# v scaled by a maximum and kept as two float16 parts, and x of some chunks handed over through DRAM, in a fused attention and two-MLP kernel

## The chip, the cores and the metric

One core of a Trainium2 chip runs the whole program. The metric is device microseconds (us) from start to end of one execution; lower is better. Of the kernel before there are three runs: a median of 1001.1 us, between 998.04 and 1001.42.

## What is computed

The reference, cut to what matters:

```python
# attention: 4 batches, 8 heads, 576 positions, 64 per head; causal
scores = q @ k.T / 8
bias = -(cum[:, :, :, None] - cum[:, :, None, :])      # cum: running sum of max(s, 0)
scores = where(causal, -1e9, scores + minimum(bias, 0))
attn = softmax(scores)
x = (attn @ v), laid out as [2304 tokens, 512]
# first MLP, 2048 wide
r = maximum(x @ w_in, 0)
x = (s * r * r + b) @ w_out
# second MLP, 1536 wide
out = ((x @ w_a) * (x @ w_b)) @ w_out2
```

All inputs of the products are float32 or float64; the kernel splits them into high and low parts and multiplies the parts, three terms to a float32 product (high x high, high x low, low x high).

## The kernel before

**Stages.** The 2304 tokens are nine chunks of 256. Chunks 0 to 3 are the first 256 positions of the four batches ("first halves"), chunks 4 to 7 the next 256 ("second halves"), chunk 8 the last 64 positions of all four batches, which are worked out with the second halves. Attention makes x of a chunk (`first_half`, `second_half`, each ending in `value_product`). The first MLP takes x: `h_unit` multiplies by w_in, `elementwise` squares, `y_unit` multiplies by w_out, chunk by chunk; chunks 7 and 8 go together with 512 columns (`last_two`). Attention of later chunks is laid between the MLP's matmuls of earlier ones. When the first MLP is done, the second MLP follows (`x_pair`, `group`, `conv`, then `g_pair`, `g_conv`).

**One value product.** A pair of heads is one product: first halves have two key blocks, second halves five. Probabilities are scaled by 32768 (PSC) and kept as two float16 parts; v is kept as three bfloat16 parts, so that their sum has v's digits. `split_v` (L356) makes them: cast, subtract, cast, subtract; the casts run on POOL for first halves and on ACT (ScalarE) for second halves, the subtractions on DVE, in place in the buffer of raw v (`rv`). `value_product` (L562) sums five terms per key block and head: three parts of v with the high part of the probabilities, two with the low part. The result lies in a bank of the tag `t_s`, the pool of four PSUM banks that scores use as well, and ACT and DVE write it out as a high and a low part of x.

**x.** `x_all` has two slots of four pairs; chunk c uses slot c mod 2, so a value product of chunk c can only run when the MLP has read chunk c − 2 (`room=[xt]`). x of chunk 8 is collected in DRAM (`xl_dr`) and read back (L825).

**What sets the order.** All work is declared with `op(engine, cost, position, ...)`. `Plan.order` (L122) replays the declared costs and positions and puts out one fixed order per engine; a buffer is given when its turn in its tag comes. On the chip each engine then works through its list in order. A DMA stands in the list of SP, which issues all of them; a waiting instruction holds up all behind it on its engine. `light_pos` (L410) gives the positions of first halves, the call of `second_half` at 130 + 78b + 19p those of the second halves. The rest of the tables here are the tags, with their number of buffers:

```python
t_h = tag(ps_mm, [P, 512], F32, 2, "h", in_order=False)      # banks of h
t_s = tag(ps_at, [P, 512], F32, 4, "s", in_order=False)      # banks of scores and value products
t_r = tag(moe, [P, 2, N], F32, 2, "r", in_order=False)       # between h and its split
t_rv = tag("att1", [P, 5, 2, D], F32, 1, "rv")               # raw v of a second half
t_vt = tag("att1", [P, 5, 2, 3, D], BF16, 1, "vt")           # its parts
```

Of the kernel before, what the change touches and what calls it, by code (L numbers as in the profile page):

```python
# [22 lines left out]
PSC = 32768.0  # L23
G_ACT = (0, 1)
# [211 lines left out]
def fused_kernel(  # L236
# [66 lines left out]
    xl_dr = dram_buf([NPAIR, P, 2, N], F32R, "xl_dr")  # L303
    y_dr = dram_buf([(NCK + 1) // 2, KC, P, 2 * N], F32, "y_dr")
# [7 lines left out]
    x_slots = iter([x_all[:, ck % 2, c] for ck in range(NCK) for c in range(KC)])  # L312
    t_x = Tag(lambda n: next(x_slots), 2 * KC)
    t_xl = tag(moe, [P, 2, SL], F32R, 2, "xl")
# [4 lines left out]
    def make_const():  # L319
        nc.gpsimd.memset(as32(ident), 0.0)  # L320
# [14 lines left out]
    mask2 = atc.tile([P, SL], F32R, name="mask2")  # L335
    sb_s = const.tile([P, 1], F32, name="sb_s")
# [12 lines left out]
    t_vt0 = tag("att0", [P, 2, 2, 2, 3, D], BF16, 2, "vt")  # L349
# [3 lines left out]
    t_sm0 = {n: tag("att0", [P, 4], F32, 3, n) for n in ("nm", "sm", "rc")}  # L353
    t_raw = tag("att0", [P, 2, DM, 2], U32, 1, "rl")

    def split_v(v3, rv, eng, cost, sub, pr):  # L356

        buf, ap = v3
        rvb, rap = rv
        cast = nc.gpsimd.tensor_copy if eng == POOL else nc.scalar.copy  # L360
        ops = []
        for i in range(2):
            ops.append(op(eng, cost, pr, lambda i=i: cast(ap(i), rap()), r=[rvb], w=[(buf, i)]))
            if i == 0:
                op(DVE, sub, pr, lambda: nc.vector.tensor_tensor(out=rap(), in0=rap(), in1=ap(0), op=ALU.subtract),
                   r=[(buf, 0)], w=[rvb])
        op(DVE, sub, pr, lambda: nc.vector.tensor_tensor(out=ap(2), in0=rap(), in1=ap(1), op=ALU.subtract),
           r=[rvb, (buf, 1)], w=[(buf, 2)])
        return ops

    light = {}
    casts = []
# [4 lines left out]
    def light_load(i, in_w):  # L377
# [6 lines left out]
        light[i] = kq, rv, vt  # L384
# [8 lines left out]
        def ones():  # L393
# [3 lines left out]
        op(POOL, 1.9, pr, ones, w=[(kq, "o0"), (kq, "o1")], behind=casts[2 * i - 3 : 2 * i - 2])  # L397
# [10 lines left out]
        casts.extend(split_v((vt, lambda a: vt.t[..., a, :]), (rv, lambda: rv.t), POOL, 0.63, 0.7, light_pos(i) + (0.5 if i else 2.6)))  # L408
# [116 lines left out]
    x_t = {}  # L525

# [35 lines left out]
    def value_product(b, half, p, vt, vap, tr, pr):  # L562
# [4 lines left out]
        ap = Buf(t_s, f"av{b}{half}{p}")  # L567
        xt = x_t[b + B * half, p]
# [28 lines left out]
    def first_half(i):  # L597

        b, g = divmod(i, 2)
        kq, rv, vt = light[i]  # L600
# [5 lines left out]
        for x in range(2):  # L606
            p = 2 * g + x
            pr = light_pos(i) + 2.5 * x
            x_t[b, p] = Buf(t_x, f"xs{b}{p}")
# [5 lines left out]
            for ti in (1, 0):  # L615
# [15 lines left out]
                op(PE, 2 * (w / 600 + 0.08), pr, go, r=[kq, masks], w=[bank], late=0.15, room=[hl])  # L631
                op(DVE, DVE_PS(2 * w), pr, lambda at=at, nmx=nmx, view=view: nc.vector.tensor_reduce(
                    out=nmx.t[:, at : at + 2], in_=view(), axis=AX.X, op=ALU.max, negate=True
                ), r=[bank], w=[(nmx, ti)])
                tiles[ti] = w, bank, at, view, hl
            op(DVE, 0.17, pr, lambda nmx=nmx: nc.vector.tensor_scalar_mul(nmx.t, nmx.t, SCALE), w=[nmx])
            pts = {}
            for ti in (1, 0):
                w, bank, at, view, hl = tiles[ti]
                for h in range(2):  # L640
# [5 lines left out]
                    ), r=[bank, nmx], w=[pt, (sm, at + h)], late=0.1)  # L646
# [10 lines left out]
            value_product(b, 0, p, vt, lambda j, h, vi, x=x: vt.t[:, x, j, h, vi, :], tr, pr + 1.0)  # L657
# [15 lines left out]
    barrier.tags = {t_kq0, t_rv0, t_vt0, t_p0, t_tr0, t_raw, *t_hl0.values(), *t_sm0.values()}  # L673
# [27 lines left out]
    t_vt = tag("att1", [P, 5, 2, 3, D], BF16, 1, "vt")  # L701
# [6 lines left out]

    def second_half(b, p, pos):
# [27 lines left out]
        split_v((vt, lambda a: vt.t[..., a, :]), (rv, lambda: rv.t), ACT, 0.7, 0.82, pos + 0.9)  # L737
# [17 lines left out]
        for z, ti in enumerate(("L", 1, 0)):  # L755
# [6 lines left out]
            for c in range(2):  # L762
                def go(c=c, ti=ti, w=w, bank=banks[c]):
# [18 lines left out]
                op(PE, 0.56 if ti == "L" else 2 * (w / 2400 + 0.014) + 0.08, pr, go, r=[sets, masks], w=[banks[c]], late=0.15,  # L782
                   room=[hl])
# [750 lines left out]
```

## Time and profile before

| | |
|---|---|
| median of 3 runs | 1001.1 us |
| profiled execution | 998.96 us, its span 997.2 us |
| PE (TensorE) busy | 968.4 us, 97% of the span |
| weight loads (PEld, beside PE) | 871.5 us, 87% |
| DVE (VectorE) | 707.4 us, 71% |
| ACT (ScalarE) | 548.9 us, 55% |
| POOL (GpSimd) | 108.5 us, 11% |
| DMA | 160.12 MB, mean 161 GB/s |

Busy time is a share of the whole span, over stages that differ. Matmuls are pipelined and their ends are modelled, so PE's share is not its distance from its peak. The chain followed back from the last instruction says what set the end; what an engine costs is read from the stage in which the work stands.

### The profile page before, as it was taken

To read this page: it belongs to the slowest core of one execution; us is meant where nothing else is said; L and a number is where in the kernel's file an instruction comes from. 1 tells how busy PE (TensorE), PEld (TensorE's weight loads), DVE (VectorE), ACT (ScalarE), POOL (GpSimd) and SP (SyncE) were. 2 spreads that over 40 slices of the span, in tenths; PEclk is the share of its full clock that TensorE was granted. 3 is DMA by queue.
4 is the path that set the end of the run, shared out by engine and by line. 5 is a ranking of instruction groups with operands and counts; after the bars stand their busy time and mean duration, and the time that the engine had idled before them with its cause. 6 is when DMAs were issued, how large, how long until landed. Compare 5 with 4: busy or idle time off the path is not lost.

```text
span 997.2 us, 17243 instructions
## 1 busy us (share of the span) xinstructions
PE 968.4 (97%) x6664; PEld 871.5 (87%) x6664; DVE 707.4 (71%) x1151; ACT 548.9 (55%) x1025; POOL 108.5 (11%) x135
## 2 busy tenths in 40 slices
PE   5798999999999999999999999999999999999998
PEld 4698999999999999999988887888888888888888
DVE  6887644578888788888576627778688776878852
ACT  4788984568778777777463423344253421334431
POOL 4121000100000000000001004133143311000000
PEclk9999999999999999999999999999999999999999
DMA  9969423457776858777560103446366556977013
GB/s 240 231 164 227 163 82 79 113 128 141 168 148 157 172 128 165 159 153 146 106 226 1 63 24 125 156 147 247 137 240 228 187 185 260 377 307 253 22 65 104
DMA packets 159249, 160.12 MB, mean 161 GB/s; under 512 B 115008, under 2 KB 126016, under 8 KB 153280
## 3 DMA queue, kind: packets, MB, share of 16 engines
q1 hardware_dynamic: 159168, 159.03, 55.9%
q8 instruction: 52, 0.85, 0.4%
q14 instruction: 29, 0.24, 0.1%
HBM read 95.20 MB, written 37.52 MB: 133 GB/s over the span
## 4 chain that ended last, share of the span: by engine, by line
PE 92%; DMA 3%; DVE 2%; ACT 1%; issue 0%; POOL 0%; SPq 0%; DVEq 0%; POOLq 0%; ACTq 0%
PE b L1100 21%; PE y L882 16%; PE h L862 15%; PE pb L1324 11%; PE av L577 6%; PE hh L915 4%; PE yy L927 4%; PE bc L1100 3%; PE s L627 3%; PE s L779 3%; PE pbc L1384 2%; DMA raw<-in_w_dram 2%; DMA tr<-hl 1%; DVE x1d L1035 1%; PE s L628 0%; DMA yr<-y_dr 0%
## 5 line engine op out<-in xcount | busy, mean ns | idle before, releaser
L882 PE MATMUL y<-g,w 128*128 128x256 f32 x1344 | 183.6, 286 | 1.8 <-ACT p L643 1.8
L862 PE MATMUL h<-x_all,w 128*128 128x256 f32 x1344 | 179.0, 285 | 2.7 <-ACT x_all L588 2.1
L862 PEld LDWEIGHTS h<-x_all,w 128*128 128x128 f32 x1344 | 167.8, 192 | 4.4 <-ACT x_all L588 2.3
L882 PEld LDWEIGHTS y<-g,w 128*128 128x128 f32 x1344 | 167.9, 191 | 3.5 <-ACT p L643 2.0
L577 PE MATMUL av<-tr,vt 128*64 128x320 f16 (+4 forms) x1120 | 64.8, 273 | 9.1 <-DMA tr<-hl 9.1
L1100 PE MATMUL b<-x,wa 128*128 128x512 f32 x288 | 72.8, 390 | 0.0
L577 PEld LDWEIGHTS <-vt 128*64 128x64 bf16 x1120 | 54.3, 115 | 20.2 <-issue 6.6
L541 ACT ACTIVATE hl<-p,rc 128x256 f16<-128x256 f32 (+3 forms) x128 | 65.5, 558 | 10.7 <-DVE rc L558 6.9
L543 DVE SCALAR_TENSOR_TENSOR hl<-p,rc,hl 128x256 f16<-128x256 f32 (+3 forms) x128 | 65.5, 549 | 1.6 <-ACT hl L541 1.3
L1100 PEld LDWEIGHTS b<-x,wa 128*128 128x128 f32 x288 | 53.6, 188 | 11.3 <-ACT su L1135 0.5
L842 DVE SCALAR_TENSOR_TENSOR r<-r,sb_s 128x512 f32<-128x512 f32 x40 | 30.0, 750 | 37.8 <-ACT r L831 37.8
L1100 PE MATMUL b<-x1d,ws 128*128 128x512 f32 x216 | 54.1, 390 | 0.6 <-DVE su L1125 0.5
L1100 PE MATMUL b<-x0d,ws 128*128 128x512 f32 x216 | 53.7, 389 | 0.0
L627 PE MATMUL s<-kq 66*128 66x256 f32 (+1 forms) x128 | 42.4, 458 | 10.2 <-DMA kq<-sums 7.8
L1324 PE MATMUL pb<-g,wo 128*128 128x512 f32 x216 | 50.7, 390 | 0.0
L1100 PEld LDWEIGHTS b<-x1d,ws 128*128 128x128 f32 x216 | 40.4, 188 | 9.7 <-DVE su L1125 1.4
L1324 PEld LDWEIGHTS pb<-g,wo 128*128 128x128 f32 x216 | 40.4, 188 | 8.7 <-DVE g L1272 0.4
L1100 PEld LDWEIGHTS b<-x0d,ws 128*128 128x128 f32 x216 | 40.4, 188 | 8.3
L463 DVE SCALAR_TENSOR_TENSOR raw<-raw 128x1024 uint32<-128x1024 uint32 x28 | 34.9, 1245 | 17.1 <-ACT raw L457 14.2
L831 ACT ACTIVATE r<-h 128x512 f32<-128x512 f32 x56 | 33.5, 598 | 24.1 <-PE h L862 22.1
L1125 DVE TENSOR_TENSOR su<-b,su 128x512 f32<-128x512 f32 x48 | 33.0, 688 | 17.9 <-PE b L1100 17.7
L915 PE MATMUL hh<-x_all,w 128*128 128x512 f32 x192 | 45.7, 389 | 0.0
(380 smaller groups left out, 1881.3 us busy)
## 6 DMA issues: line engine op xcount, KB each, us to landing
raw<-in_w_dram SPq DMA_DIRECT2D x16, 1024.0 KB
raw<-in_w2ab_dram SPq DMA_DIRECT2D x12, 1024.0 KB
ab_dr<-at_all SPq DMA_DIRECT2D x24, 512.0 KB
R<-ab_dr SPq DMA_DIRECT2D x24, 512.0 KB
wo<-wo_dr SPq DMA_DIRECT2D x12, 1024.0 KB
rk<-in_k_dram SPq DMA_DIRECT2D x16, 576.0 KB
raw_o<-in_w2o_dram SPq DMA_DIRECT2D x6, 1024.0 KB
wo_dr<-wao SPq DMA_DIRECT2D x24, 256.0 KB
```

Of the source, the lines that this page charges most:

```text
L463: op(DVE, 1.15, pr, lambda: nc.vector.scalar_tensor_tensor(out=hi(), in0=hi(), scalar=3, in1=lo(), op0=ALU.logical_shift_left, op1=ALU.bit ...
L541: nc.scalar.activation(o, i_, AF.Copy, scale=r_)
L543: nc.vector.scalar_tensor_tensor(out=o, in0=i_, scalar=r_, in1=place()[:, k0:k1, 0, :cols], op0=ALU.mult, op1=ALU.subtract)
L577: nc.tensor.matmul(ap.t[64 * h : 64 * h + 64, :w], vap(j, h, vi), t[:, j, a, h, :w], start=j == 0 and m == 0, stop=j == nkt - 1 and m == 4,)
L627: nc.tensor.matmul(o, qt[:66, x, h, ti * P : (ti + 1) * P], kt[:66, x, h, :w], start=True, stop=False)
L831: op(ACT, 0.49, e, lambda: nc.scalar.activation(r.t.rearrange("p a n -> p (a n)"), hp.t, AF.Relu), r=[hp], w=[r], late=0.1)
L862: nc.tensor.matmul(o, w[:, wi, c, :], x_t[ck, c].t[:, xi], start=m == 0, stop=m == 3 * KC - 1)
L882: nc.tensor.matmul(o, w1_t[2 * fp + j].t[:, 1, wi, e * P : (e + 1) * P], g.t[:, gi, j], start=fp == 0 and e % 2 == 0 and j == wi == gi == ...
L915: nc.tensor.matmul(hp.t, w[:, wi, c, :], x_all[:, :, c, xi, :], start=m == 0, stop=m == 3 * KC - 1)
L927: nc.tensor.matmul(y_ps[e].t, w1_t[f].t[:, 1, wi, e * P : (e + 1) * P], g.t[:, gi].rearrange("p a n -> p (a n)"), start=f == m == 0, stop= ...
L1100: nc.tensor.matmul(o, wt.t[:, q, wi, kt * P : (kt + 1) * P], hl_of(kt, xi), start=first and n == 0, stop=last and n == 5, skip_group_check ...
L1324: nc.tensor.matmul(banks[bi][dp].t, wv(i2, wi, dp), hl.t[:, i2, xi, :], start=n_ in fresh and ip == i2 == m == 0, stop=ip == NIP - 1 and i ...
```

## The change

**Scale and parts of v.** For each block of v, DVE takes the largest absolute value in each partition; one float32 matmul with a matrix of 1/32768 (`ones`) adds these over the partitions and puts the sum into every partition, in column 511 of a score bank; three small DVE operations make of it the factor for v, and the factor that goes back on when x is written out. v times the factor is kept as two float16 parts (one cast, one subtraction), and a value product sums three terms: high x high, low x high, high x low.

**Where value products of second halves go.** Into a bank of `t_h` and no longer of `t_s`.

**x.** Pairs outside the set `DIRECT` (all of chunks 2, 3 and 7, pairs 1 to 3 of chunk 4, pair 3 of chunk 6: 16 pairs) are written into an `r` buffer, from there to DRAM (`xs_dr`), and read into their slot when it is free. x of chunks 7 and 8 has a tile of its own (`x_end`), in space that attention leaves at its end, and is read back from DRAM by eight loads. The raw weights of the second MLP take the space of `x_all` instead.

**Positions.** First halves 4 to 7 stand at 44 + 12(i − 4) (50 + 14(i − 4) before), second halves at 110 + 80b + 19p (130 + 78b + 19p before). The work of chunks 7 and 8 is declared matmul group by matmul group, in the same count and shape.

The diff, cut to its core:

```diff
+VSC = 32768.0
-    x_slots = iter([x_all[:, ck % 2, c] for ck in range(NCK) for c in range(KC)])
+    x_slots = iter([x_all[:, ck % 2, c] for ck in range(NCK - 2) for c in range(KC)])
...
+    t_xe = Tag(end_slot, 2 * KC)
...
+        nc.gpsimd.memset(ones, 1.0 / VSC)
...
-    t_vt0 = tag("att0", [P, 2, 2, 2, 3, D], BF16, 2, "vt")
+    t_vt0 = tag("att0", [P, 2, 2, 2, 2, D], F16, 2, "vt")
...
+    def scale_v(vs, mx, rv, bank, n, pr):
+
+        op(DVE, DVE_1(n) + 0.25, pr, lambda: nc.vector.tensor_reduce(
+            out=mx.t, in_=rv[1](), axis=AX.X, op=ALU.max, apply_absolute_value=True
+        ), r=[rv[0]], w=[mx])
+        col = slice(511, 512)
+        op(PE, 0.1, pr, lambda: nc.tensor.matmul(bank.t[:, col], ones, mx.t, start=True, stop=True, skip_group_check=True),
+           r=[mx, masks], w=[(bank, "v")], late=0.1)
+
+        def go():
+            nc.vector.tensor_scalar_max(vs.t[:, 0:1], bank.t[:, col], 1e-30)
+            nc.vector.reciprocal(vs.t[:, 1:2], vs.t[:, 0:1])
+            nc.vector.tensor_scalar_mul(vs.t[:, 2:3], vs.t[:, 0:1], 1.0 / PSC)
+
+        op(DVE, 0.5, pr, go, r=[(bank, "v")], w=[vs])
+
-    def split_v(v3, rv, eng, cost, sub, pr):
+    def split_v(v2, rv, vs, eng, cost, sub, pr):
...
+            if eng == POOL:
+                nc.gpsimd.tensor_scalar(ap(0), rap(), vs.t[:, 1:2], None, op0=ALU.mult)
+            else:
+                nc.scalar.activation(ap(0), rap(), AF.Copy, scale=vs.t[:, 1:2])
+
+        op(DVE, sub, pr, lambda: nc.vector.scalar_tensor_tensor(
+            out=ap(1), in0=rap(), scalar=vs.t[:, 1:2], in1=ap(0), op0=ALU.mult, op1=ALU.subtract
+        ), r=[rvb, vs, (buf, 0)], w=[(buf, 1)], after=[c := op(eng, cost, pr, cast, r=[rvb, vs], w=[(buf, 0)])])
...
-        return 0.0 + 5.0 * i if i < 2 else 14.0 + 9.0 * (i - 2) if i < 4 else 50.0 + 14.0 * (i - 4)
+        return 0.0 + 5.0 * i if i < 2 else 14.0 + 9.0 * (i - 2) if i < 4 else 44 + 12 * (i - 4)
...
+    DIRECT = {(ck, p) for ck in range(NCK - 2) for p in range(NPAIR)} - {(2, 0), (2, 1), (2, 2), (2, 3), (3, 0), (3, 1), (3, 2), (3, 3), (4, 1), (4, 2), (4, 3), (6, 3)}
...
-        ap = Buf(t_s, f"av{b}{half}{p}")
-        xt = x_t[b + B * half, p]
+        ck = b + B * half
+        away = (ck, p) not in DIRECT
+        ap = Buf(t_h if half else t_s, f"av{b}{half}{p}")
+        xt = Buf(t_r, f"xw{ck}{p}") if away else x_t[ck, p]
...
-                for m, (vi, a) in enumerate(((0, 0), (1, 0), (2, 0), (0, 1), (1, 1))):
+                for m, (vi, a) in enumerate(((0, 0), (1, 0), (0, 1))):
...
+        if away:
+            op(SP, 0.4, pr, lambda: nc.sync.dma_start(as32(xs_dr.t[ck - 2, p]), xt.t), r=[xt], w=[(xs_dr, (ck, p))], dma=262144)
...
+                scale_v(vs, mx, (rv, lambda: rv.t.rearrange("p c h d -> p (c h d)")), banks[0], 640, pos + 0.15)
+                split_v((vt, lambda a: vt.t[..., a, :]), (rv, lambda: rv.t), vs, ACT, 0.7, 0.82, pos + 0.9)
...
-            second_half(b, p, 130.0 + 78.0 * b + 19.0 * p)
+            second_half(b, p, 110 + 80 * b + 19 * p)
...
+        op(SP, 0.4, pr, lambda: nc.sync.dma_start(as32(x_t[ck, p].t), as32(xl_dr.t[p] if last else xs_dr.t[ck - 2, p])),
+           r=[xl_dr if last else (xs_dr, (ck, p))], w=[x_t[ck, p]], dma=262144)
```

Names in the rows below: `hC_F`, `yC_E` are the MLP's products of chunk C; `av` with batch, half and pair is a value product; `s` with half, batch, pair and tile a score bank (`L` is the block of the last 64 positions); `mx` the new maximum; `rv`, `tr`, `raw` are raw v, transposed probabilities and raw w1.

PE's order around the first scores of second half (batch 1, pair 0), before:

```order
L862 MATMUL h3_5_3538<-x_all_82,w1_10_1310 128x256 x12
L769 MATMUL s110L0_3556<-K0_2414,Q0_2413 128x288 x2
L769 MATMUL s110L0_3556<-K1_2416,Q1_2415 128x288 x2
L769 MATMUL s110L1_3564<-K0_2414,Q0_2413 128x288 x2
L769 MATMUL s110L1_3564<-K1_2416,Q1_2415 128x288 x2
L775 MATMUL s110L1_3564<-mask2_85,ident_83 128x64
L882 MATMUL y3_1_3229<-g3_2_3227,w1_4_601 128x256 x3
L882 MATMUL y3_1_3229<-g3_2_3227,w1_5_896 128x256 x3
L862 MATMUL h3_5_3538<-x_all_82,w1_11_1458 128x256 x12
```

and in the change:

```order
L934 MATMUL h3_4_3376<-x_all_83,w1_8_1164 128x256 x12
L827 MATMUL s110L0_3401<-K0_2223,Q0_2222 128x288 x2
L827 MATMUL s110L0_3401<-K1_2225,Q1_2224 128x288 x2
L827 MATMUL s110L1_3402<-K0_2223,Q0_2222 128x288 x2
L827 MATMUL s110L1_3402<-K1_2225,Q1_2224 128x288 x2
L833 MATMUL s110L1_3402<-mask2_86,ident_84 128x64
L934 MATMUL h3_4_3376<-x_all_83,w1_9_1317 128x256 x12
L954 MATMUL y3_0_3177<-g3_2_3236,w1_4_775 128x256 x3
L954 MATMUL y3_0_3177<-g3_2_3236,w1_5_942 128x256 x3
L376 MATMUL s110L0_3401<-mx110_3434,ones_87 128x1
L954 MATMUL y3_1_3187<-g3_2_3236,w1_4_775 128x256 x3
L954 MATMUL y3_1_3187<-g3_2_3236,w1_5_942 128x256 x3
```

The value product `av012` stands four `y3` products (2.88 us) ahead of the first row; the new matmul on `mx110` stands behind the scores, an h product and six `y3` matmuls, and the rest of PE's list behind it.

SP's order around the load of v for batch 0, pair 3 (`rv103`), before:

```order
L594 DMA xl_dr_80<-xl01_3244 256x1x64
L718 DMA rq110_3296<-in_q1_dram 128x704
L749 DMA_TRANSPOSE tr102_3224<-hl1020_2949 128x12x128
L719 DMA rv103_3339<-in_v_dram 128x640
L720 DMA Q1_2415<-aug_q_78 2x2x320
L723 DMA K1_2416<-aug_k_79 2x2x576
```

and in the change:

```order
L640 DMA xs_dr_81<-xw41_2961 128x512
L642 DMA xl_dr_80<-xl01_3014 256x1x64
L801 DMA_TRANSPOSE tr102_3066<-hl102L_2900 128x10x64 x2
L888 DMA x_all_83<-xs_dr_81 128x512
L778 DMA rv103_3102<-in_v_dram 128x640
L777 DMA rq110_3104<-in_q1_dram 128x704
L776 DMA rk110_3113<-in_k_dram 128x1152
```

The load of v now stands behind the write of a pair of x to DRAM and directly behind a reload of x.

SP's order at the fourth and fifth loads of w1, before:

```order
L653 DMA_TRANSPOSE tr002_352<-hl0021_193 128x8x128
L653 DMA_TRANSPOSE tr002_352<-hl0020_206 128x4x128
L448 DMA raw4_375<-in_w1_dram 128x2048
L520 DMA aug_q_78<-sums_hl_275 16x2x64
L520 DMA aug_q_78<-sums_hl_275 16x2x256
L400 DMA kq4_394<-in_kl_dram 64x1024
L400 DMA kq4_394<-in_ql_dram 64x1024
L448 DMA raw3_432<-in_w1_dram 128x2048
```

and in the change:

```order
L433 DMA rv04_453<-in_v_dram 128x2x256
L437 DMA kq4_328<-sums_107 1x4x256 x2
L432 DMA kq5_477<-in_kl_dram 64x1024
L709 DMA_TRANSPOSE tr010_488<-hl0101_355 128x8x128
L709 DMA_TRANSPOSE tr010_488<-hl0100_372 128x4x128
L432 DMA kq5_477<-in_ql_dram 64x1024
L433 DMA rv05_536<-in_v_dram 128x2x256
L437 DMA kq5_477<-sums_107 1x4x256 x2
L709 DMA_TRANSPOSE tr011_575<-hl0111_383 128x8x128
L709 DMA_TRANSPOSE tr011_575<-hl0110_431 128x4x128
L479 DMA raw3_608<-in_w1_dram 128x2048
L479 DMA raw4_610<-in_w1_dram 128x2048
```

These two loads of w1 now stand behind the transposes of three more pairs (`tr003`, which is just ahead of the rows, `tr010` and `tr011`) and behind the loads for `kq5`.

## Rows read from the trace of the kernel before

**Rows 1.** The page: its part 1, and the chain of part 4 by line.

```profile
PE 968.4 (97%) x6664; PEld 871.5 (87%) x6664; DVE 707.4 (71%) x1151; ACT 548.9 (55%) x1025; POOL 108.5 (11%) x135
...
PE b L1100 21%; PE y L882 16%; PE h L862 15%; PE pb L1324 11%; PE av L577 6%; PE hh L915 4%; PE yy L927 4%; PE bc L1100 3%; PE s L627 3%; PE s L779 3%; PE pbc L1384 2%; DMA raw<-in_w_dram 2%; DMA tr<-hl 1%; DVE x1d L1035 1%; PE s L628 0%; DMA yr<-y_dr 0%
```

**Rows 2.** Busy time by stretch: length, engines (instructions), granted clock, DMA share, GB/s.

```profile
0.00:56.00 56.00, 36.65 (x192) 30.95 (x193) 39.79 (x88) 33.98 (x92) 17.92 (x30) 1.00 0.94 241
56.00:104.00 48.00, 43.47 (x372) 41.43 (x371) 38.03 (x77) 42.39 (x105) 6.77 (x9) 1.00 0.76 203
104.00:509.00 405.00, 405.00 (x3777) 392.11 (x3776) 292.38 (x584) 293.72 (x610) 9.32 (x25) 1.00 0.61 139
```

**Rows 3.** Pieces of the chain in order of time: start us, us, what.

```profile
48.39 1.81 PE av L577 x20
...
61.27 0.94 PE av L577 x20
...
74.59 7.71 DMA raw<-in_w_dram
...
85.70 0.43 PE s L627 x2
...
86.74 0.27 PE s L627 x2
...
248.09 2.73 PE av L577 x50
...
256.23 1.06 PE s103L L769 x8
...
258.83 1.44 PE y L882 x12
260.27 0.47 PE s L779 x2
...
264.27 2.73 PE av L577 x50
...
491.64 2.73 PE av L577 x50
...
508.95 10.91 PE hh L915 x48
```

**Rows 4.** Timeline: DVE's splits of v and SP's load of the next.

```profile
254.00 0.83 DVE L365 TENSOR_TENSOR rv<-rv,vt 128x640 f32<-128x640 f32 x1 [0.23 <-ACT vt L363]
...
267.80 0.83 DVE L365 TENSOR_TENSOR rv<-rv,vt 128x640 f32<-128x640 f32 x1 [0.52 <-ACT vt L363]
...
270.99 0.82 DVE L367 TENSOR_TENSOR vt<-rv,vt 128x640 bf16<-128x640 f32 x1
274.43 0.53 SPq L719 DMA_DIRECT2D rv<-in_v_dram  x1
```

**Rows 5.** DVE's groups of instructions: busy us, mean ns, then idle before.

```profile
L784 DVE TENSOR_REDUCE nm<-s 128x1 f32<-128x512 f32 x32 | 21.0, 687 | 1.9
...
L784 DVE TENSOR_REDUCE nm<-s 128x1 f32<-128x384 f32 x32 | 16.6, 551 | 0.7 <-PE s L780 0.7
...
L461 DVE TENSOR_SCALAR raw<-raw 128x1024 uint32<-128x1024 uint32 x14 | 10.5, 752 | 5.3 <-DMA raw<-in_w_dram 4.4 <-DMA raw<-in_w2ab_dram 0.8
...
L558 DVE RECIPROCAL rc<-rc 128x2 f32<-128x2 f32 x32 | 5.3, 166 | 1.1
```

**Rows 6.** Busy time from 225 to 475 us (columns as in rows 2).

```profile
225.00:475.00 250.00, 250.00 (x2364) 240.23 (x2363) 207.98 (x433) 194.16 (x415) 2.88 (x14) 1.00 0.72 153
```

**Rows 7.** The chain again: waits for reads of 256 KB.

```profile
612.46 3.97 DMA yr<-y_dr
...
623.08 2.62 DMA yrc<-y_dr
```

**Rows 8.** SP's timeline near the last write and the reloads of x.

```profile
495.57 0.53 SPq L594 DMA_DIRECT2D xl_dr<-xl  x1
...
499.26 3.19 SPq L825 DMA_DIRECT2D x_all<-xl_dr  x4
```

More of the change, by code (lines that the diff above doesn't have):

```diff
@@ L353, in fused_kernel, with cast @@
     t_sm0 = {n: tag("att0", [P, 4], F32, 3, n) for n in ("nm", "sm", "rc")}
+    t_mx0, t_vs0 = tag("att0", [P, 1], F32, 2, "mx"), tag("att0", [P, 3], F32, 3, "vs")
     t_raw = tag("att0", [P, 2, DM, 2], U32, 1, "rl")
-    def split_v(v3, rv, eng, cost, sub, pr):
-        buf, ap = v3
-        rvb, rap = rv
[L360 to L369, printed above, removed]
+    def scale_v(vs, mx, rv, bank, n, pr):
[11 more added lines that the diff above has]
+    def split_v(v2, rv, vs, eng, cost, sub, pr):
+        buf, ap = v2
+        rvb, rap = rv
+        def cast():
+            if eng == POOL:
[5 more added lines that the diff above has]
+        ), r=[rvb, vs, (buf, 0)], w=[(buf, 1)], after=[c := op(eng, cost, pr, cast, r=[rvb, vs], w=[(buf, 0)])])
+        return c
     light = {}
-    casts = []
+    fills = []
     last_rows = []
@@ L391, in light_load, with fill @@
         hs = slice(b * H + 4 * g, b * H + 4 * g + 4)
-        def ones():
+        def fill():
             nc.gpsimd.memset(view()[64:66, 1], 1.0 / SCALE)
             nc.gpsimd.memset(view()[64:66, 0], -1.0 / SCALE)
-        op(POOL, 1.9, pr, ones, w=[(kq, "o0"), (kq, "o1")], behind=casts[2 * i - 3 : 2 * i - 2])
+        fills.append(op(POOL, 1.9, pr, fill, w=[(kq, "o0"), (kq, "o1")]))
         for j, src in enumerate((kl, ql)):
@@ L645, in first_half @@
                         accum_out=sm.t[:, at + h : at + h + 1],
[L646 removed]
+                    ), r=[(bank, "s"), nmx], w=[pt, (sm, at + h)], late=0.1)
             recip(rc, sm, pr)
@@ new lines, in fused_kernel, with h_wide, go @@
+    wide_g, wide_y = {}, {}
+    def h_wide(cks, f, pr):
+        t_ = f"{cks[0]}_{f}"
+        hp, g, r = Buf(t_h, f"hh{t_}"), Buf(t_g, f"gg{t_}"), Buf(t_r, f"rr{t_}")
+        for c in range(KC):
+            def go(c=c):
+                x_ = (x_end[0] if cks[0] == NCK - 2 else x_all)[:, :, c]
+                w = w1_t[f].t[:, 0].rearrange("p a (c f) -> p a c f", c=KC)
+                for m, (wi, xi) in enumerate(((0, 0), (0, 1), (1, 0))):
+                    nc.tensor.matmul(hp.t, w[:, wi, c, :], x_[:, :, xi, :], start=c == m == 0, stop=c == KC - 1 and m == 2)
+            op(PE, 0.69, M + pr, go, r=[w1_t[f], *(x_t[ck, z] for ck in cks for z in range(KC))], w=[hp], late=0.15)
+        elementwise(hp, g, r, pr - M, False)
+        wide_g[cks, f] = g
@@ L1001, in after @@
                 o.wait += 1
+    for o in end_loads:
+        ready2[0].next.append(o)
+        o.wait += 1
     ring = {}
```

190 lines of the change are left out of this document (109 added, 81 removed).

## Prediction, made before the change was run

> **What bounds the kernel now.** I read the page first, then a table of stages, then the chain of waits. The page [rows 1] has TensorE (PE) busy for 968.4 of 997.2 us. A reader should distrust "busy" (a matmul's end is modelled) and trust the chain that ends last: nearly all of it is lines of PE, and value products, `av`, are 6.1% of the span, 60.8 us. The stages [rows 2] say where such work counts. From 104 us on PE has no idle time, 405.00 of 405.00 us up to the last pair of chunks, so each matmul that goes is time gained there. From 0 to 104 us it is idle for 104 − 36.65 − 43.47 = 23.9 us: that stretch is set by transposes, by loads of w1 and by ScalarE, which is busy for 42.39 of 48 us from 56 to 104. The profiled execution took 998.96 us for a span of 997.2; it lies 2.1 under the median of 1001.1 and 0.9 over the lowest run. My sum starts from 998.96.
>
> **Part 1: five terms become three.** A first-half value product falls from 20 matmuls to 12, a second-half one from 50 to 30. The shapes stay and both operands have 16 bits before and after, so I scale the blocks of the chain by 3/5. A second-half block takes 2.73 us [rows 3], 16 of them: 16 x 2.73 x 2/5 = **−17.5 us**. Of the 16 first-half products the last 8, those of batches 2 and 3, run after 104 us; at 0.94 us a block [rows 3] they give 8 x 0.94 x 2/5 = **−3.0 us**. The other 8 run before 104 us. There a block takes 1.81 us at 48.39 and 0.94 at 61.27 [rows 3], about half as long for the same work: the granted clock reads 1.00 for the whole stretch [rows 2], but the durations are those of its two levels, 1.2 and 2.4 GHz; between the two blocks PE ran value products, scores and the first h products without a gap. Five blocks at the low level and three at the high one would give 5 x 0.72 + 3 x 0.38 = 4.7 us if PE set the pace there. It mostly does not.
>
> **Part 2: the front.** Two things move besides. x of chunks 2 and 3 no longer waits for the slots of chunks 0 and 1, so first halves of batches 2 and 3 can fill PE's gaps (4.5 us of them between 56 and 104 us [rows 2]). Against that SP's order puts the fourth and fifth loads of w1 behind three more pairs of transposes, and one wait for a w1 load stands with 7.71 us in the chain [rows 3]. Also eight writes and reloads of x go through SP here. Best: 4.7 + 4.5 = 9.2 us gained. Worst: one more such wait, 7.7 us lost. I take **−2 us**, nearer to zero than to either, because ScalarE's work in this stretch is hardly touched: v is cast on POOL here, once where it was twice.
>
> **Part 3: the scale.** Each of the 24 blocks of v gets a maximum: a DVE reduction, one float32 matmul with a single column on PE, three tiny DVE operations. No such matmul is in the trace. A float32 product runs as two matmuls: 0.43 us at 256 columns and 0.27 at 128 [rows 3], a line that meets one column at 0.11. I take 0.13 (its weights follow each other with nothing to hide behind); 0.11 and 0.27 are the ends: 24 x 0.13 = **+3.1 us** (2.6 to 6.5).
> On DVE one of two subtractions (0.83 us [rows 4]) goes, the other stays; the reduction and three operations of 0.166 us [rows 5] come. For the reduction over 640 elements there are two kinds of row: a one-source operation from SBUF, 1024 elements in 0.752 us, would make it 0.47; reductions from PSUM, 0.551 us at 384 and 0.687 at 512, make it 0.82 [rows 5]. I take 0.82, since it is the same operation. The Trainium skill, "VectorE: DVE Perf Modes" (The perf-mode tier table), says that a reduction has only its slowest form wherever its data lie, while one-source operations on SBUF have faster ones; by that it is 0.82, by the SBUF row 0.47, and the chain below would be 0.35 us shorter. DVE then works 0.82 + 0.50 − 0.83 = 0.5 us more for each second half. From 225 to 475 us it is busy for 207.98 of 250 us [rows 6]; some 14 second halves add 7 us and PE's work there shrinks by 14, so its share goes from 83% to about 91%. I cost that at nothing: PE is then still the fuller of the two.
>
> **Part 4: what waits for the maximum.** The new matmul stands in PE's order, and everything behind it waits with it; DVE's reduction likewise waits in order for the load of v. There is one buffer for raw v. So before product n's maximum come: the cast of n−1 (which needs the end of value product n−2), its one subtraction, SP's turn, the load, the reduction. From rows: subtraction done 1.63 us after the value product (267.80 + 0.83 against 264.27 + 2.73); SP's turn 2.62 us later (270.99 + 0.82 to 274.43) [rows 3, 4]; issue 0.53; landing 2.62 to 3.97, the chain's waits for 256 KB reads [rows 7], say 3.3; reduction 0.82. Together **8.9 us**. I counted, in the change's PE order, the work between the end of value product n−2 and maximum n, at 1.44 us per 12 matmuls of h or y, 1.06 for a left-over score block and 0.47 for a score pair [rows 3]: 7.3 us in the case shown ahead of this text (2.88 + 1.44 + 1.06 + 1.44 + 0.72, less roundings), 9.4 to 10.3 in five, 12.2 to 14.3 in the other eight. Only the first waits: **+1.7 us**. Without SP's turn and with the fast ends, 5.3 us, nothing waits. With the slow cast (254.00 + 0.83 against 248.09 + 2.73 makes 4.0 [rows 3, 4]) and landing 3.97 it is 11.9 us, and the waits add up to 15.
>
> **Part 5: x and the tail.** Value products of second halves now end in the two banks of h, and sixteen x pairs pass through the two `r` buffers to DRAM. A write of x stands before its reload on SP: from the last write of `xl` (495.57) to the first reload (499.26) it was 3.7 us, and four reloads took 3.19 us to issue [rows 8]. Before the last pair of chunks there are now eight reloads: 3.7 + 2 x 3.19 + 4 = 14 us behind the last write, which itself follows the last value product by 3.9 us (495.57 − 491.64 [rows 3, 8]). PE has about 14 us of other work there before the first product of those chunks and 4 us before that needs the last pair: 18 against 18. Covered, barely; if the cover goes the price is the rest of a transfer, 4 us at most. Behind it the kernel is the same work in the same order. I put both at 0.
>
> **The sum:** −17.5 − 3.0 − 2 + 3.1 + 1.7 = −17.7. 998.96 − 17.7 = 981.3; the median lay a little higher than this execution, and I say **982 us**. A difference under 0.5% (5 us) can't be told from none with these measurements.
>
> **Rivals.**
> *A, the wait for v takes the place of the work (slower).* If the chain of part 4 takes over 12.5 us in every product, the waits eat all 19.4 us that the rest gives; at 14 us they are 35 us and the time 999 − 19.4 + 35 = 1015. Place: the new matmul on PE, 14 second halves. For it: v's load is late in SP's order, now twice directly behind a reload of x that waits for its own write, and DVE stalls with PE. Against it: the rows give 11.9 us at worst, and PE did not wait once from 104 to 509 us.
> *B, the clock.* PE's bursts in the first 56 us get shorter by two fifths of their value products and its gaps longer. If it comes to the high level 10 us later, half of 10 us is lost: 987. The row is that of part 1: the level rose after a stretch without a gap. The Trainium skill, "TensorE: Matmul & The Clock Gate" (Part 1), says that the low level is the state at rest and that sustained activity lifts it; by that rule less work at the start can cost time. The trace agrees as far as 1.81 against 0.94 us goes.
> *C, the front fills.* With x free of slots, the gaps of part 2 close: 982 − 7 = 975.
> *D, most of the gain is eaten* by DVE at 91%, by h waiting for a bank that a value product holds, and by the hand-over of part 5: half the saving, 991 to 998. The change then does what it says and PE simply waits elsewhere.
>
> **How the numbers follow.** The forecast (976 to 989) has 0.60, B 0.10, C 0.10, D 0.11, A 0.09. Faster by over 0.5% means under 996: the forecast, B, C and most of D, 0.87. Within 0.5%: the rest of D and the edge of A, 0.05. Slower: 0.08. The best sum is −17.5 − 3.0 − 9.2 + 2.6 = −27, 972; the worst end of the waits alone (+15 for +1.7) gives 995. The range, **970 to 997**, holds both and leaves out A.
>
> **What would show it.** Value-product blocks of 1.64 us in the chain after 104 us and about 0.55 for first halves; 24 one-column matmuls of 0.1 to 0.2 us; PE idle after 104 us in the table of waits at the new line, 2 us in all; the first wide h product near 491 us instead of 508.95 [rows 3], and from there to the end the same 488 us. I am wrong if PE's waits at that line exceed 10 us (A), if blocks of 1.8 us are found after 60 us (B), or if the part behind the last pair of chunks has grown.

## The result, and the profile after

| | before | changed kernel |
|---|---|---|
| median | 1000.7 us (11 executions, 997.4 to 1001.9) | 1005.9 us (11, 1001.5 to 1009.4) |
| profiled execution, its span | 998.96, 997.2 us | 1008.28, 1006.5 us |
| PE busy in it | 968.4 us | 965.5 us |

The ratio is 1.0054, with a 95% interval of 1.0035 to 1.0072. The change makes the kernel half a per cent slower. The forecast was 982 us, 18 faster; its range ended at 997.

The page of the changed kernel, its part 1 (against [rows 1]) and the chain of part 4 by engine; the last line is that chain before:

```profile
PE 965.5 (96%) x6264; PEld 869.5 (86%) x6264; DVE 715.8 (71%) x1223; ACT 545.4 (54%) x1009; POOL 113.3 (11%) x128
...
PE 72%; DMA 7%; ACT 4%; DVE 3%; issue 2%; SPq 1%; POOL 0%; ACTq 0%; POOLq 0%; DVEq 0%
...
PE 92%; DMA 3%; DVE 2%; ACT 1%; issue 0%; POOL 0%; SPq 0%; DVEq 0%; POOLq 0%; ACTq 0%
```

PE's share of the chain has fallen from 92% to 72%. Four hundred matmuls are gone, but PE is busy for only 3 us less, and its idle time has grown from 28.8 to 1006.5 − 965.5 = 41.0 us. Both have to be explained. The stages of the changed kernel, with the columns of [rows 2] (the last row is the stretch of [rows 6]):

```profile
0.00:56.00 56.00, 39.50 (x185) 34.26 (x186) 39.36 (x103) 31.62 (x95) 20.66 (x27) 1.00 0.80 183
56.00:104.00 48.00, 42.18 (x292) 39.76 (x291) 34.74 (x75) 39.01 (x85) 8.37 (x7) 0.79 0.82 234
104.00:515.00 411.00, 398.43 (x3448) 386.61 (x3448) 301.78 (x638) 291.98 (x605) 8.38 (x22) 1.00 0.68 158
225.00:475.00 250.00, 237.85 (x2086) 229.76 (x2085) 202.87 (x443) 180.55 (x381) 2.86 (x14) 0.99 0.73 158
```

From 104 us to the first wide h product, 405.00 us without a gap before, the stretch is now 411 us and PE stands idle for 12.6 of them. From 56 to 104 us the granted clock is 0.79, so work there takes longer without being more. That is where the busy time went: up to 104 us PE is busy for 39.50 + 42.18 = 81.7 us, 1.6 more than before, and gets less done. It has run 118 matmuls of h and 72 of y by then (the same view, of these tiles alone), against 156 and 90 before; the 56 that are missing, at 1.44 us for 12 [rows 3], are 6.7 us of work that now stands behind 104 us. Against that stand two more first-half value products (0.62 us each in the chain after 104 us) and a few matmuls of scores. Pieces of the chain in order of time show that two of the terms came out near the forecast:

```profile
231.28 1.70 PE av L620 x30
...
246.81 0.13 PE s102L L376 x2
...
254.23 7.85 DMA y_dr<-yo
```

A value product of a second half takes 1.70 us (2.73 before [rows 3]; 1.64 was forecast) and the one-column product 0.13 us, to the digit. What is new is the rest of the chain, which before was PE's work and nothing else in this stretch. The changed kernel's table of waits says who stands (engine, line, what it waited for: us in total, times, longest), first of PE from 104 to 515 us, its four longest rows, then of DVE and of ACT from 225 to 515 us:

```profile
PE av L620 <- DMA tr<-hl: 4.5, 5, 1.8
PE s L837 <- DVE vs L380: 2.5, 1, 2.5
PE s130L L376 <- DVE mx L372: 1.8, 1, 1.8
PE s111L L376 <- DVE mx L372: 1.6, 1, 1.6
```

```profile
DVE mx L372 <- DMA rv<-in_v_dram: 12.3, 9, 2.6
```

```profile
ACT r L903 <- DMA y_dr<-yo: 6.8, 2, 4.8
```

PE's rows sum to 10.4 of its 12.6 us: 5.9 behind instructions of the maximum, 4.5 at value products that wait for transposed probabilities. VectorE stands nine times for the load of v whose maximum is next in its order, and ScalarE's relu stands for one of the two `r` buffers. One place, read in the timelines of four engines of the changed kernel, shows how a wait off PE's own path gets to PE. First SP, then ACT (start us, us, line, operation, and in brackets the idle time before it):

```profile
251.28 0.58 SPq L888 DMA_DIRECT2D x_all<-xs_dr  x1
251.98 0.37 SPq L778 DMA_DIRECT2D rv<-in_v_dram  x1
252.45 1.25 SPq L777 DMA_DIRECT2D rq<-in_q_dram  x1
253.79 0.38 SPq L776 DMA_DIRECT2D rk<-in_k_dram  x1
254.23 0.43 SPq L967 DMA_DIRECT2D y_dr<-yo  x1
```

```profile
262.16 0.60 ACT L903 ACTIVATE r<-h 128x512 f32<-128x512 f32 x1 [4.83 <-DMA y_dr<-yo]
262.66 0.49 ACT L859 ACTIVATE p103L<-s103L,nx103L 128x288 f32<-128x288 f32 x1
```

then DVE, then PE:

```profile
256.99 0.82 DVE L372 TENSOR_REDUCE mx<-rv 128x1 f32<-128x640 f32 x1 [0.87 <-DMA rv<-in_v_dram]
...
263.28 0.16 DVE L380 TENSOR_SCALAR vs<-s103L 128x1 f32<-128x1 f32 x1 [3.86 <-ACT p103L L859]
```

```profile
263.49 1.00 PE L837 MATMUL s<-K,Q 128*128 128x384 f32 x2 [2.48 <-DVE vs L380]
```

Four loads issued within 3 us stand ahead of the write of `yo`, which lands 7.85 us after its issue. Until then the relu has no `r` buffer. Behind it on ScalarE waits the exponential of the next block, behind that VectorE's small step L380, which takes the maximum out of the bank of these scores, and for that step PE's next scores wait: 2.48 us of idle PE. The reduction itself took the 0.82 us that was chosen from [rows 5]; DVE's share from 225 to 475 us is 202.87 of 250, 81% and not the 91% expected: the same work did not get packed into a shorter time, and 13 maxima fall into these 250 us.

### The profile page after: what moved, and what is told of

It reads as the page before. It is cut to its first block, busy times and chain, and to the rows that moved or that the text cites. A ratio compares the mean times of both kernels' runs of the same rounds, so it can differ in the third digit from the quotient of the medians.

```text
span 1006.5 us, 16535 instructions
## 1 busy us (share of the span) xinstructions
PE 965.5 (96%) x6264; PEld 869.5 (86%) x6264; DVE 715.8 (71%) x1223; ACT 545.4 (54%) x1009; POOL 113.3 (11%) x128
## 4 chain that ended last, share of the span: by engine, by line
PE 72%; DMA 7%; ACT 4%; DVE 3%; issue 2%; SPq 1%; POOL 0%; ACTq 0%; POOLq 0%; DVEq 0%
PE b L1182 20%; PE pb L1406 11%; PE y L954 11%; PE h L934 10%; PE hh L982 4%; PE av L620 3%; PE bc L1182 3%; DMA tr<-hl 2%; PE yw L997 2%; PE yy L997 2%; PE s L837 2%; PE pbc L1466 2%; DMA rv<-in_v_dram 1%; DMA y_dr<-yo 1%; DMA raw<-in_w_dram 1%
## 5 line engine op out<-in xcount | busy, mean ns | idle before, releaser
L934 PE MATMUL h<-x_all,w 128*128 128x256 f32 x1344 | 182.8, 291 | 1.9 <-DVE w L503 1.7
L954 PE MATMUL y<-g,w 128*128 128x256 f32 x1344 | 180.9, 286 | 0.0
L934 PEld LDWEIGHTS h<-x_all,w 128*128 128x128 f32 x1344 | 172.3, 197 | 3.3 <-DVE w L503 2.0
L620 PE MATMUL av<-tr,vt 128*64 128x320 f16 (+4 forms) x672 | 41.9, 276 | 14.7 <-ACT hl L582 5.5
L620 PEld LDWEIGHTS <-vt 128*64 128x64 f16 x672 | 34.8, 116 | 22.5 <-issue 13.1
L982 PE MATMUL hh<-x_end,w 128*128 128x512 f32 x192 | 52.5, 389 | 0.0
L674 PE MATMUL s<-kq 66*128 66x128 f32 (+1 forms) x128 | 47.1, 497 | 2.9 <-ACT p L699 1.5
L859 ACT ACTIVATE p<-s,nm 128x512 f32<-128x512 f32 (+1 forms) x64 | 40.2, 630 | 11.9 <-DVE vs L380 4.2
L1207 DVE TENSOR_TENSOR su<-b,su 128x512 f32<-128x512 f32 x48 | 33.0, 687 | 18.8 <-PE b L1182 18.6
L1217 ACT COPY su<-b 128x512 f32<-128x512 f32 x24 | 14.1, 587 | 53.0 <-PE b L1182 53.0
```

Of the source, the lines that this page charges most:

```text
L620: nc.tensor.matmul(ap.t[64 * h : 64 * h + 64, :w], vap(j, h, vi), t[:, j, a, h, :w], start=j == 0 and m == 0, stop=j == nkt - 1 and m == 2,)
L674: nc.tensor.matmul(o, qt[:66, x, h, ti * P : (ti + 1) * P], kt[:66, x, h, :w], start=True, stop=False)
L859: nc.scalar.activation(pt.t[:, lo : lo + w], bank.t[:, :w], AF.Exp, bias=mm, scale=1.0, accum_out=sm.t[:, c : c + 1])
L934: nc.tensor.matmul(o, w[:, wi, c, :], x_t[ck, c].t[:, xi], start=m == 0, stop=m == 3 * KC - 1)
L954: nc.tensor.matmul(o, w1_t[2 * fp + j].t[:, 1, wi, e * P : (e + 1) * P], g.t[:, gi, j], start=fp == 0 and e % 2 == 0 and j == wi == gi == ...
L982: nc.tensor.matmul(hp.t, w[:, wi, c, :], x_[:, :, xi, :], start=c == m == 0, stop=c == KC - 1 and m == 2)
```

## The experiments

**First, which part costs?** Four kernels separate the scale from x's way through DRAM. The first is the kernel before with the value part alone:

```
-    t_vt = tag("att1", [P, 5, 2, 3, D], BF16, 1, "vt")
+    t_vt = tag("att1", [P, 5, 2, 2, D], F16, 1, "vt")
+    t_mx, t_vs = tag("att1", [P, 1], F32, 2, "mx"), tag("att1", [P, 3], F32, 3, "vs")
...
-                for m, (vi, a) in enumerate(((0, 0), (1, 0), (2, 0), (0, 1), (1, 1))):
+                for m, (vi, a) in enumerate(((0, 0), (1, 0), (0, 1))):
```

> The kernel before with the value part of the change alone: v scaled by its maximum, two float16 parts, three terms; x, the s banks of the products and the placing of second halves stay as before. Theory 1 (the wait for the maximum eats the gain: VectorE stands in the second halves for the load of rv): 992 to 999 us. Rival (x's way through DRAM, the new banks and the placing eat it, and the scale costs what was forecast): 979 to 986 us, with the stretch from the first second-half value product to the first wide h product 14 us or more below the 279.9 us of before.

1019.7 us, ratio 1.020 (1.018 to 1.022): slower than either theory had it.

```
-    ones = atc.tile([P, P], F32, name="ones")
+    vs_t = atc.tile([P, 3], F32, name="vs_t")
...
-        nc.gpsimd.memset(ones, 1.0 / VSC)
+        nc.gpsimd.memset(vs_t[:, 1:2], VSC / 8.0)
+        nc.gpsimd.memset(vs_t[:, 2:3], 8.0 / VSC / PSC)
...
```

> As the run with the value part alone, but the scale is a constant 4096 in place of the maximum, so that there is no reduction, no one-column product and no wait for them. Theory 1: 978 to 984 us (the 20.5 us of matmuls that the third part cost, all on the path). Rival (VectorE or the loads set the pace of the second halves once the products are shorter, whatever the scale): 990 to 998 us.

985.4 us, ratio 0.986 (0.984 to 0.988), between the two ranges and nearer theory 1. Three terms are worth 14.3 us, and the maximum 34 us when nothing else of the change is there. The same edit in the changed kernel:

> The changed kernel with a constant scale of 4096 in place of the maximum; all else of the change stays. Theory 1: 989 to 993 us (12.3 us of VectorE's wait for rv and 3.1 us of one-column products go), with no wait of VectorE on rv's load over 1 us a piece. Rival (x's way and the placing): 1001 to 1004 us, only the 3.1 us of products go.

993.0 us, ratio 0.993 (0.991 to 0.994): the maximum costs 1005.9 − 993.0 = 12.9 us here. The time lies at the end of theory 1's range, but the runs below show that VectorE's waits are not the whole reason. And the changed kernel with x straight to its place:

```
-    DIRECT = {(ck, p) for ck in range(NCK - 2) for p in range(NPAIR)} - {(2, 0), (2, 1), (2, 2), (2, 3), (3, 0), (3, 1), (3, 2), (3, 3), (4, 1), (4, 2), (4, 3), (6, 3)}
+    DIRECT = {(ck, p) for ck in range(NCK - 2) for p in range(NPAIR)}
```

> The changed kernel with every x of chunks 0 to 6 written straight to its place, none through DRAM; the scale, the banks and the placing of the change stay. Theory 1: 1002 to 1005 us (only the wait of ScalarE's relu for the r buffers goes, some 3 us of it on the path). Rival (x's way): 988 to 994 us.

1021.4 us, ratio 1.021 (1.019 to 1.023): not 3 us faster but 15.5 slower, at about the time of the value part alone (1019.7). With the maximum, x's way through DRAM is worth 15.5 us. PE's table of waits says how, first in this kernel, then in the value part alone:

```profile
PE hh L982 <- DMA x_end<-xs_dr: 15.1, 1, 15.1
...
PE hh L950 <- DMA x_all<-xl_dr: 14.8, 1, 14.8
```

The chain of the value part alone shows what stands ahead:

```profile
511.91 2.96 PE av L598 x28
...
520.06 9.53 DMA x_all<-xl_dr
529.59 0.04 issue
529.63 10.57 PE hh L950 x39
```

The last value product comes at 511.91 us there (at 511.34 in the changed kernel without trips) and nothing is left for PE between it and the first wide h product. Before, 14.6 us of narrow h and y stood there (491.64 + 2.73 to 508.95 [rows 3]) and covered the write and reload. The work that fills PE while second halves wait had run out, since they took longer. The wait costs more than itself: behind it the granted clock stands at 0.50 from 528 to 531 us, in the kernel without trips, and the first 24 wide products take 8.01 us in its chain where they take 5.47 in the changed kernel's.

**Second, is it the load, the buffer, the clock?** Each from the changed kernel.

```
-    t_rv = tag("att1", [P, 5, 2, D], F32, 1, "rv")
+    t_rv = tag("att1", [P, 5, 2, D], F32, 2, "rv")
```

> The changed kernel with a second buffer for the v of a second half, of which the planner knows, so that v's load no longer waits for the split of the block before; the order of the second halves shifts a little with it. Theory 1 (VectorE, standing for that load 12.3 us in 9 waits, holds the second halves back): 994 to 999 us, with those waits under 2 us in all. Rival (they stand beside TensorE's other work, and the loss is the clock and the front): 1003 to 1007 us.

999.8 us, ratio 1.001 (0.999 to 1.002): between the two ranges, 6 us gained where theory 1 had 7 to 12. VectorE's waits for v fell from 12.3 to 6.8 us. The order changed too, so the gain is not the buffer's alone.

```
+    t_rv = Tag(lambda n: pools["att1"].tile([P, 5, 2, D], F32, tag="rv", bufs=2, name=n), 1)
```

> The changed kernel with the same second buffer, but the planner is not told, so that every engine's order is that of the changed kernel and only the load's wait for the buffer goes. Theory 1: 996 to 1001 us. Rival A (the load's turn in SyncE's queue, not the buffer, makes it late): 1004 to 1007 us and the 12.3 us of waits stay.

1009.4 us, ratio 1.008 (1.006 to 1.011), above both ranges, and the waits are those of the changed kernel:

```profile
DVE mx L372 <- DMA rv<-in_v_dram: 12.9, 9, 2.5
```

This is what the run's rival A said of the waits: a free buffer does nothing while the load has its old turn on SP.

```
+            if (b, half, p) == (1, 0, 2):
+                for _ in range(48):
+                    nc.tensor.matmul(HP[0, 1].t[:, 256:384], ident, mask1, start=True, stop=True, skip_group_check=True)
...
```

> The changed kernel with 48 matmuls of 128 columns whose result is overwritten, put on TensorE ahead of the one first-half value product that waited 3.2 us at 66 to 69 us, after which the granted clock stood at 0.50 until 81 us; the order is otherwise the same. Theory 2 (the clock's fall after the gap costs some 6 us that come back at the end): 998 to 1002 us and a granted clock of 1.00 up to 81 us. Rival (the second halves are held by their loads and take back what the front gains): 1004 to 1007 us, with the clock at 1.00 all the same.

1007.4 us, ratio 1.007 (1.005 to 1.010). The stretches 66 to 69, 69 to 81 and 81 to 84 us, first of the changed kernel, then of this one:

```profile
66.00:69.00 3.00, 0.00 (x1) 0.11 (x1) 3.00 (x6) 2.57 (x6) 0.00 (x0) 0.94 1.13 381
69.00:81.00 12.00, 11.80 (x58) 11.27 (x58) 11.50 (x22) 10.09 (x24) 1.84 (x2) 0.50 0.86 222
81.00:84.00 3.00, 3.00 (x28) 2.80 (x27) 0.72 (x3) 2.18 (x8) 0.00 (x0) 0.79 0.80 253
```

```profile
66.00:69.00 3.00, 3.00 (x29) 3.00 (x29) 3.00 (x5) 2.60 (x6) 0.00 (x0) 1.00 1.01 313
69.00:81.00 12.00, 10.73 (x95) 9.87 (x94) 10.55 (x23) 10.51 (x28) 2.63 (x3) 1.00 0.85 210
81.00:84.00 3.00, 1.29 (x17) 0.82 (x16) 1.94 (x3) 3.00 (x6) 1.02 (x1) 1.00 0.77 313
```

The clock falls to 0.50, the low level of 1.2 GHz, after the gap, and it does not fall where the gap is filled. But what starts at 87.80 us in the changed kernel starts at 84.00 here, and at the end nothing is left of that: theory 2 falls, its rival stands. One caveat belongs here. The fill lasted 5.5 us where the gap was 3.2, and the mean granted clock over all executions hardly moved (median 0.994, changed kernel 0.995): filling one gap leaves the others. Still, the profiled execution had a mean clock of 0.998 and took 1005.3 us, so a high clock alone does not bring the time back.

> The changed kernel with the constant scale and every x of chunks 0 to 6 straight to its place. Theory 3 (x's way through DRAM frees TensorE's work for the time that the maximum holds the second halves back, and costs otherwise): 984 to 988 us, at the time of the value part with the constant. Rival (the way through DRAM is worth its 15 us whatever the scale, as it was with the maximum): 1004 to 1010 us.

984.7 us, ratio 0.986 (0.983 to 0.988). Theory 3 holds: with the constant, DRAM costs 993.0 − 984.7 = 8.3 us; with the maximum it is worth 15.5.

**Third, the value of the scale or the work for it?**

```
-                nc.scalar.activation(ap(0), rap(), AF.Copy, scale=vs.t[:, 1:2])
+                nc.scalar.activation(ap(0), rap(), AF.Copy, scale=vs_c[:, 1:2])
...
```

> The changed kernel, order and work the same, but the split of v and the writing out of the products take a constant 4096 as scale: the maximum, the one-column product and the three small steps still run, and nothing waits for what they give. Theory 1a (VectorE stands for v's load in its order, TensorE for the column): 1003 to 1007 us, the 12.3 us of VectorE's waits stay. Theory 1b (the chain load, maximum, column, scale, split, product is what is too long): 993 to 997 us.

1008.7 us, ratio 1.007 (1.006 to 1.009), above both ranges. Nobody needs the scale, and nothing is gained: 1b falls. This is not yet the chain of the forecast's part 4, which ends at the new matmul. Load, reduction and that matmul still run here and still hold up what stands behind them: VectorE waits 13.1 us for v, PE 4.8 us at the new matmul after 104 us.

```
...
-        op(SP, 0.4, lp, lambda: nc.sync.dma_start(rv.t, v[b, p]), w=[rv], dma=327680, after=opened, slack=True)
+        op(SP, 0.4, lp - 19.0, lambda: nc.sync.dma_start(rv.t, v[b, p]), w=[rv], dma=327680, after=opened, slack=True)
```

> The changed kernel with the second buffer for v, known to the planner, and v's load given the priority of the block before, so that v has landed when its maximum is due. Theory 1 (the load's lateness is what the maximum costs): 992 to 997 us, the time with the constant and 3.1 us for the one-column products, with VectorE's waits for v under 2 us in all. Rival (other links of the maximum's chain hold it): 999 to 1004 us, as with the second buffer alone.

999.7 us, ratio 1.000 (0.998 to 1.002), in the rival's range. VectorE's waits for v are down to 1.6 us (225 to 515 us), and PE has none at the new matmul after 104 us; VectorE's longest now include

```profile
DVE r L914 <- ACT r L903: 16.3, 8, 4.5
DVE xw L636 <- ACT xl L634: 5.6, 6, 2.9
DVE nm L842 <- PE s L838: 3.8, 8, 0.6
```

Yet the time is that of the second buffer alone. The load's lateness accounts for about half of the maximum's price at most, since the order changed with it.

> As the run before, and every x of chunks 0 to 6 straight to its place. Theory 3 (the way through DRAM pays only while the maximum holds the second halves back): 985 to 991 us, faster than both kernels with the maximum kept. Rival (the last second half still comes after the other work has run out): 1005 to 1020 us with a wait ahead of the first wide h product.

1014.8 us, ratio 1.014 (1.013 to 1.016): the rival. With the maximum the last second half comes too late even when v is early, and the first wide h product waits 16.4 us for its reload.

**Fourth, the work or the order?** The same order of every engine's other work, without the maximum's own:

```
-        op(PE, 0.1, pr, lambda: nc.tensor.matmul(bank.t[:, col], ones, mx.t, start=True, stop=True, skip_group_check=True),
+        op(PE, 0.1, pr, lambda: None,
...
```

> The changed kernel in its own order, with a constant 4096 as scale and the work for the maximum left out: no reduction, no one-column product, no three small steps. Theory 1a (VectorE's standing for v and the work itself cost the 13 us that the constant saves): 991 to 996 us. Rival (the order that the planner makes for the maximum is what costs, whoever waits): 1002 to 1007 us.

997.8 us, ratio 0.999 (0.997 to 1.000), between the two. Of the 12.9 us, 1005.9 − 997.8 = 8.1 are the work and the waits that it brings; 997.8 − 993.0 = 4.8 are the order that the planner makes when it thinks each second half longer. What the 8.1 consist of is not shown. In its profile PE is idle for 11.8 us from 104 us to the first wide h product, hardly less than the 12.6 of the changed kernel, 8.3 of them at value products that wait for transposed probabilities: the waits at the maximum went and others came.

```
+    DIRECT = {(ck, p) for ck in range(NCK - 2) for p in range(NPAIR) if ck != 2}
```

> The run with the second v buffer and the early load, the maximum kept, and only chunk 2's x through DRAM instead of 12 pieces of chunks 2, 3, 4 and 6. Theory 4 (chunk 2 alone has to get out of the first halves' way; each further trip through the r buffers only costs): 992 to 997 us, faster than both kernels. Rival (the trips are free once v is early): 999 to 1003 us.

995.9 us, ratio 0.996 (0.994 to 0.999): theory 4, at its slow end. Chunk 2's trips alone are worth 1014.8 − 995.9 = 19 us with the maximum. It is the only kernel with the maximum kept that is faster than both, by 0.4% against before. With the constant:

> The changed kernel with the constant scale and only chunk 2's x through DRAM. Theory 4: 983 to 988 us, since chunks 3, 4 and 6 no longer take r buffers in the second halves. Rival (chunk 2's own trip is the cost): 991 to 995 us.

990.5 us, ratio 0.990 (0.989 to 0.991), between the two ranges and close to the rival's: the four trips of chunk 2 cost 990.5 − 984.7 = 5.8 us, the other eight 2.5. And with a buffer of its own:

```
-        xt = Buf(t_r, f"xw{ck}{p}") if away else x_t[ck, p]
+        xt = Buf(t_xw[half], f"xw{ck}{p}") if away else x_t[ck, p]
...
```

> The changed kernel with the constant scale, and a buffer of its own for the x that goes through DRAM, so that relu's r buffers no longer wait for those writes. Theory 4 (the 8 us that the way through DRAM costs with the constant is the sharing of the two r buffers): 985 to 989 us. Rival (it is the writes, the reloads and their turns in SyncE's queue): 991 to 995 us.

1001.4 us, ratio 1.001 (0.999 to 1.003), above both ranges and 8.4 us slower than with the shared buffers. One buffer of its own is less than a share of two. This doesn't decide whether the sharing is what costs; a test with a third `r` buffer wasn't made.

The fastest kernels are the two with the constant and no trip, 985 us, but 4096 holds only while v times 4096 fits into a float16, as it does for these inputs (v is normal with a spread of 0.1), and the maximum needs no such condition.

## Why the prediction was wrong

A ledger of medians, each step one experiment: the changed kernel 1005.9; without the maximum's work 997.8; in the order planned without it 993.0; without trips 984.7. The forecast, 982 with 4.8 us for the scale, puts that last kernel at 977. So the error of 24 us is 8.1 us (12.9 for 4.8) on the maximum, 8.3 (for 0) on x's way, and 7.5 on the rest. The ledger has two limits. The runs were made at different times, in which the median of the kernel before went from 999.6 to 1000.7 us; by the ratios the three steps are 6.9, 5.9 and 7.0 us. Three experiments in the changed kernel's own order lie 0.2 to 0.3% above it, so a step of 2 or 3 us says nothing. And the steps depend on the order in which they are taken: without trips the maximum costs 1021.4 − 984.7 = 36.7 us, of which the trips then give 15.5 back.

**Part 1 was right, as a term.** Blocks of 1.70 us (1.68 to 1.77 elsewhere in the chain), first halves 0.62 where 0.55 was expected; PE's busy time with the constant and no trip is 946.9 us, 21.5 under that of before, where 20.5 and some of the front's 4.7 were expected. But its span is only 14.6 us shorter: PE idles 982.6 − 946.9 = 35.7 us there, 6.9 more than before: 0.6 up to 104 us, 2.7 from there to the first wide h product, 3.7 behind it. So "each matmul that goes is time gained there" held but for 2.7 us without maximum and trips. In the changed kernel, with 12.6 us of idle PE in that stretch, it failed: 405.00 us without a gap showed that PE was never short of work, not that the other engines could keep up with less of it.

**Part 2, the front: −2 forecast.** In the changed kernel it went the other way: 6.7 us of narrow h and y moved behind 104 us, in an execution whose clock was the lowest of eleven. In the kernel with the constant and no trips PE's idle time in the first 104 us is 24.5 us, against 23.9 [rows 2]:

```profile
0.00:56.00 56.00, 34.74 (x157) 29.26 (x158) 38.45 (x86) 34.64 (x97) 19.18 (x28) 1.00 0.91 221
56.00:104.00 48.00, 44.75 (x360) 42.95 (x359) 36.02 (x72) 42.87 (x96) 7.13 (x6) 0.96 0.81 224
104.00:490.00 386.00, 383.35 (x3375) 373.25 (x3374) 281.36 (x562) 288.25 (x594) 9.97 (x23) 1.00 0.66 148
```

The front is paced by transposes, loads and ScalarE, as the text said. Up to the first wide h product this kernel gains 508.8 − 490.0 = 18.8 us, not the 22.5 of −17.5, −3.0 and −2; behind it, it takes 492.6 us instead of 488.4, with 2.5 us of waiting for ScalarE at a wide product. ScalarE's relu stands there behind its work on raw weights of the second MLP (`raw_all`), which now lie in the space of `x_all`; the chain has 8.56 us of their load at 486.91 us. These 3.7 and 4.2 us are the rest of the ledger.

**Part 3: right in its prices, 0.13 and 0.82 us.** The Trainium skill, "VectorE: DVE Perf Modes" (The perf-mode tier table), had the reduction in its slowest form; the row at 256.99 agrees with 0.82 us. The share of 91% on DVE was wrong.

**Part 4 is the step that failed, in what it left out.** It counted one wait, that of PE at the new matmul, and put all other waits for the maximum at nothing. The wait that it counted came out near: 3.8 us at L376 after 104 us (1.8, 1.6 and 0.4) for the 1.7 forecast. The whole maximum, priced at 3.1 + 1.7 = 4.8 us, cost 12.9 in the changed kernel and 36.7 without trips. The buffer in its chain did not decide either: with a second one in the same order v comes as late as before (12.9 us of waits), so it is the load's turn on SP that makes it late. What runs show in place of the 4.8 us is a sum: 8.1 us go with the maximum's instructions and 4.8 more with the order planned for them. Through which waits the 8.1 reach PE stays open. The timelines above show one way, 2.48 us long: a late write holds ScalarE, ScalarE holds L380, and L380 holds PE's next scores; no experiment isolates it. Two sums of this part are slightly off, without effect: 8.9 − 7.3 is 1.6, and the fast chain comes to 5.6 us from the rows shown.

**Part 5 failed twice.** "Covered, barely" was right by itself: in the changed kernel PE has no wait at the first wide h product. But trips were not free, and their use was not seen: they keep filling work for the end. The part "same work in same order" behind that product grew from 488.4 to 491.9 us. Of this 2.4 us is y work that stood ahead of it before (0.15 us of narrow y after it then, 2.58 now), and most of the rest waits in the b products, of the changed kernel

```profile
PE b L1182 <- DVE u L1207: 1.4, 1, 1.4
```

where before the same wait was 0.8 us; all waits there together are 2.2 us against 1.3.

**The rivals.** A named the sign, the engine and the place (v's load late in SP's order, DVE and PE standing), but its mechanism, a chain over 12.5 us in every product with all of the loss at the new matmul, did not come: PE waits 3.8 us there, in three products. It had 0.09. B, the clock, is seen and small. Executions of the changed kernel had a mean granted clock of 0.988 to 0.997, those of before 0.995 to 1.000. The six at 0.995 or more took 1001.5 to 1005.9 us, the five below 1006.1 to 1009.4. The profiled one has 0.988, so its 0.79 from 56 to 104 us probably shows more than a usual execution loses. Between those two groups lie some 4 us: little of the 24 by which the forecast missed, but most of the 5 by which the change is slower than the kernel before. D came nearest to what happened without the maximum.

## What to carry to other kernels

An engine that is never idle may be kept so by filler: ask how much filler is left at the end before you count its shorter work as time, since the filler runs out sooner when the work that it covers takes longer. A small step put into an in-order queue can cost more than its own duration or its own data path: ask also who stands behind it on that engine and what it holds (a score bank, an `r` buffer). Parts of a change may have opposite worth together and alone: DRAM trips were worth +15.5 us with the maximum and −8.3 without.

## What was not expected of the hardware

After 2.5 us without work, from 261.0 to 263.5 us, PE came back at the low clock; busy time of the changed kernel by stretch:

```profile
260.00:263.00 3.00, 1.01 (x6) 0.66 (x4) 0.00 (x0) 0.84 (x2) 0.00 (x0) 1.00 0.52 119
263.00:266.00 3.00, 2.51 (x9) 2.51 (x10) 2.62 (x10) 2.29 (x8) 0.00 (x0) 0.53 1.10 243
```

The Trainium skill, "TensorE: Matmul & The Clock Gate" (Part 1), says that the low level is the state at rest; these rows agree. And a write of 256 KB took 7.85 us to land behind four loads, 1.5 MB in all, issued in the 3 us before it.
